# Output and late-query products cut into two 64-row halves that share one PSUM bank, with a TensorE drain between the halves

## The chip, the core and the metric

The kernel runs on one core of a Trainium2 chip. The metric is the device time of one execution in microseconds (us), as the median of several runs. Unless marked ns, all times below are us. Engines are named as the profile names them: PE is TensorE's matmul, PEld its weight load, DVE is VectorE, ACT is ScalarE, POOL is GpSimd, SP is SyncE, which issues most of the DMAs.

## The reference, cut to what matters

Two attention blocks over 2048 tokens of width 512, with 32 heads of 16 dimensions each, are mixed by a gate. Block A is full softmax attention. Block B is causal softmax attention inside four segments of 512 tokens, with a compressive memory of the earlier segments.

```python
x = A_x                                          # [1, 2048, 512]
g = sigmoid((x * gate_w).sum(-1, keepdims=True))
# A: q, k, v = split(x @ A_wqkv) into 32 heads of 16
a = merge(softmax(q @ k.T * 16**-0.5) @ v) @ A_wo
# B: the same inside each segment s of 512 tokens, causal, and a memory of earlier segments
p = softmax(q_s @ k_s.T * 16**-0.5 + causal)
o_s = sig(beta) * (phi(q_s) @ M) / (phi(q_s) @ z + 1e-6) + (1 - sig(beta)) * (p @ v_s)
M, z = M + phi(k_s).T @ v_s, z + phi(k_s).sum(0)
b = merge(o) @ B_wo
out = g * a + (1 - g) * b
```

## The kernel before

All products that need float32 accuracy are made of two numbers for each operand, a high and a low half (`halved[...]`), and three products: low by high, high by low, high by high.

**A first part** (up to about 280 us) computes q, k and v and the memory of block B. A **main part** follows, which is what the change is about. It walks through a list `slots` of 2368 score tiles: 32 units of block A (8 groups of four heads by 4 query chunks of 512), with 64 slots each, and 32 units of block B with 10 slots each. In a slot `n`:

- `score_part` (line 1030) makes one 128x512 score tile with a matmul over 50 rows (line 1045; two smaller matmuls in some slots of B) into a tile `st`, one of three PSUM banks, and lets ACT take the exponential into a tile `p` (line 1068).
- `max_part` (line 263) makes, 96 slots ahead (`LEAD`), a score tile of 48 rows (line 242) into `sm`, one of four PSUM banks, from which DVE takes row maxima (line 275; line 290 for the masked tiles of B). The bank is the one that was read longest ago.

Scores and maxima use 50 and 48 of 64 rows of the TensorE array. Two heads lie in rows 0 to 63 and two in rows 64 to 127 (`rows`, line 199), and the order of slots is such that a score in one half stands beside a maximum in the other.

Three slots make a **burst** (`BURST`). At the end of a burst, the loop (line 1328) gives PE further work:

- normally `some_values` (line 1080), the products of `p` and `v`: matmuls of 128 rows by 17 columns, four heads side by side, that accumulate in one bank, `ops`. When a unit is done, `ops` is copied to `oraw` by ACT (line 1106) and stored.
- if the list `shared` has entries, three of them in place of values. An entry is one matmul of 128 rows, 128 columns and 512 elements into the same bank `ops`, through the helper `matmul` at line 153 (its instructions all show as line 155). Twelve of them make one 128x512 tile, which ACT then copies out of the bank: four bursts for each tile.

`shared` is filled inside `some_values` just after a unit of block A is done, behind the copy to `oraw`. In the first 8 units of A it is filled by `later_tile` (line 958: one 128x512 tile of the queries of chunks 2 and 3), and in 22 later units by `output` (line 1241: 128 rows of the final projection, half of its terms at a time, so that `keep` copies a first half to `part` and `leave` copies the second to `res`). The list is emptied before the unit's successor is done, so that a tile's four bursts follow the unit's end directly.

The order of the instructions of an engine is the order in which this code records them.

Of the kernel before, what the change touches and what calls it, by code (L numbers as in the profile page):

```python
# [10 lines left out]
F32 = mybir.dt.float32  # L11
F32R = mybir.dt.float32r
AF = mybir.ActivationFunctionType
ALU = mybir.AluOpType
# [8 lines left out]
CH = 512  # L23
# [11 lines left out]
LEAD = 96  # L35
BURST = 3
# [3 lines left out]
NP = 6  # L40
# [7 lines left out]
def gated_mix(ctx, tc, x, xT, wqkv, a_wo, b_wq, b_wk, b_wv, b_wo, beta, gate_w, out):  # L48
# [104 lines left out]
    def matmul(*args, **kw):  # L153

        behind[0] = nc.tensor.matmul(*args, **kw)  # L155
# [149 lines left out]
    def run_todo(m):  # L305

        for e in [e for e in todo if e[0] <= m]:
            todo.remove(e)
            e[1]()
# [645 lines left out]
    def x_later(c):  # L955
        return xT[:, c * CH:(c + 1) * CH]

    def later_tile(c, o):

        def done():  # L960
            full = fr.tile([128, CH], F32, tag="part", name="full")
            nc.scalar.copy(full, ops)
            t = fr.tile([128, 2, 2, 2, 128], F32R, tag="blk", name="qhalves", bufs=2)
            t = t.rearrange("p a o h t -> p a (o h t)")
            nc.gpsimd.tensor_copy(t[:, 0], full)
            nc.gpsimd.tensor_sub(t[:, 1], full, t[:, 0].bitcast(F32))
            for i in range(2):
                at(n + 12, lambda i=i: nc.sync.dma_start(
                    qd["A", o, c][16 * i:16 * i + 16].rearrange("d h t -> (d h) t"), raw(t[:, i])))


            if o == NO - 1 and c == LATER[0]:
                for i in range(2):
                    load_halves(("x", LATER[1]), "B", x_later(LATER[1]), (2 * i, 2 * i + 1), n + 2 + 18 * i,
                                [n + 24 + 29 * i, n + 28 + 29 * i])
            elif o == NO - 1:
                for i, (side, w) in enumerate((("A", a_wo), ("B", b_wo))):
                    load_halves(side, side, w, (0, 1), n + 2 + 18 * i, [n + 22 + 8 * i, n + 26 + 8 * i])
                    for k in range(2, 4):
                        load_halves(side, side, w, (k,), n + 50 + 22 * i + 3 * (k - 2), [n + 62 + 18 * i + 5 * (k - 2)])  # L980

        def f(i):
            k, (a, b) = i // 3, ((1, 0), (0, 1), (0, 0))[i % 3]
            assert {("q", k), (("x", c), k)} <= ready
            matmul(ops, halved["q"][:, k, a, o * 128:(o + 1) * 128], halved["x", c][:, k, b],
                             start=(i == 0), stop=(i == 11))
            if i == 11:
                done()
        for i in range(12):
            yield lambda i=i: f(i)  # L990

    vt = {}

# [33 lines left out]

    queue = []

    def score_part(n):  # L1030

        u, j = slots[n]
        side, g, c = u
        q = qt[u]

        if j % 4 == 0:
            pt_[u, j // 4] = pp.tile([128, 4, CH], F32, tag="p", name="p")
            order_p[u, j // 4] = len(order_p)
            assert not queue or order_p[queue[0][1], queue[0][2] // 4] > len(order_p) - 1 - NP
        p = pt_[u, j // 4]  # L1040
        h = (0, 2, 1, 3)[j % 4]

        def score(ps, h, b, k, n0, q0):

            nc.tensor.matmul(ps[:, n0:n0 + CH - q0], rows(k[:, :, b * 128:(b + 1) * 128], h, 50),  # L1045
                             rows(q[:, :, q0:], h, 50), start=True, stop=True)

        def diagonal(x):
            nc.gpsimd.affine_select(out=x, in_=x, pattern=[[0, 4], [1, 128]], base=0, channel_multiplier=-1,  # L1049
                                    compare_op=ALU.is_ge, fill=0.0)  # L1050

        ps = banks[1 + n % BURST] if n in wide and n // BURST % 2 else st_ps.tile([128, CH], F32, tag="st", name="st")
        if side == "A":
            score(ps, h, j // 4 % 4, kt_[u, j // 16], 0, 0)
        else:
            k = kt_[u, c]
            if j < 8:
                score(ps, h, j // 4, k, 0, 128 * (j // 4))
                if j >= 4:
                    score(ps, h, 3, k, 384, 384)  # L1060
            else:
                for f in range(2):
                    score(ps, 2 * (j - 8) + f, 2, k, 256 * f, 256)
        if side == "B" and j >= 8:
            nc.scalar.activation(p[:, 2 * (j - 8):2 * (j - 8) + 2, 0:256], ps.rearrange("p (h t) -> p h t", h=2), AF.Exp,
                                 scale=SCALE)
        else:
            nc.scalar.activation(p[:, h], ps, AF.Exp, scale=SCALE)  # L1068
        if j % 4 == 3 or j == SLOTS[side] - 1:
            if side == "B":  # L1070
                diagonal(p[:, :, 0:128])
                if j == 7:
                    diagonal(p[:, :, 384:])
            queue.extend((n + (2 * BURST * (1 + (side == "B")) if n in wide else GAP[side]), u, i) for i in range(j // 4 * 4, j + 1))


    PIECES = ([(0, 128 * i, 128 * i) for i in range(4)] + [(1, 128 * i, 128 + 128 * i) for i in range(3)] + [(3, 384, 384)]
# [137 lines left out]
    def products(ps, t, b, side, o, start, stop):  # L1215

        assert (side, o) in ready
        for i, (x, w) in enumerate(((1, 0), (0, 1), (0, 0))):
            yield lambda i=i, x=x, w=w: matmul(ps, t[:, b, x], halved[side][:, o, w], start=start and i == 0,
                                                         stop=stop and i == 2)  # L1220

    def out_rows(c, b):
        return out[c * CH + b * 128:c * CH + (b + 1) * 128, :]
# [17 lines left out]
    def output(c, b, pairs, then, ps=ops):  # L1241

        ks = [(os, o, i) for os in pairs for o in os for i in range(2)]
        for k in ks:
            def f(n, k=k):
                os, o, i = k
                assert loaded_blocks[c, b, os] > len(blocks) - 2
                t = blocks[loaded_blocks[c, b, os] - 1][:, i, o % 2].unsqueeze(1)
                list(products(ps, t, 0, "AB"[i], o, k == ks[0], k == ks[-1]))[n]()
                if k == ks[-1] and n == 2:  # L1250
                    then(ps, c, b)
            for n in range(3):
                yield lambda n=n, f=f: f(n)

    part = {}

# [67 lines left out]
        return MOST + (left - 4 >= (MOST + 0.5) * runs and (due > 2 * MOST or runs == 1))  # L1324

    filled = [0]
    n = 0
    while n < nS or queue or beside or filled[0] < len(fill):
        for f in beside.pop(n, []):
            f()  # L1330
        if n < nS:
            score_part(n)
        m = n + LEAD
        if m < nS:
            loads(m + PRE)

            b = oldest()
            max_part(m, lambda: banks[b], b)
        run_todo(m)
        if n >= nS or n % (2 * BURST if n in wide else BURST) == (2 * BURST if n in wide else BURST) - 1:  # L1340
            taken = 0
            if shared:
                for _ in range(3):
                    shared.pop(0)()
            else:
                taken = some_values(n, 8 if n >= nS or n in wide else most(n))
            if n < 5:


# [59 lines left out]
```

## Time and profile before

| | us |
|---|---|
| median of 3 runs | 1745.3 (1744.92 to 1745.94) |
| span of the profiled execution | 1744.5 |
| PE busy | 1738.4 |
| PEld busy | 885.8 |
| DVE busy | 1597.1 |
| ACT busy | 1436.5 |
| POOL busy | 736.5 |

The span reaches from the first to the last instruction of one profiled execution. PE's busy time is no measure of its use, since the ends of matmuls are modelled and matmuls overlap. What a stretch costs is read from the starts of successive matmuls. Rows of the timeline give a start in us from the span's beginning, a duration in us, the engine, the line, the operation, what it writes and reads (with shapes, partitions x elements), how many instructions are merged in the row, and in brackets for how long the engine was idle before and what ended that.

### The profile page before, as it was taken

How to read it: one execution, taken by the hardware profiler on the slowest of the kernel's cores; microseconds unless marked ns; L12 is line 12 of the kernel's file. 1: busy time of each engine (PE TensorE's matmuls, PEld its weight loads, DVE VectorE, ACT ScalarE, POOL GpSimd, SP SyncE). 2: the span in 40 equal slices, each digit the busy share in tenths (PEclk: the TensorE clock that was granted, in tenths of full speed). 3: DMA queues.
4: the chain of work that ended last, by engine and by line, in shares of the span. 5: the costliest groups of instructions: out<-in, count | busy, mean ns of one | idle time of the engine just before them, and what ended most of it. 6: DMA issues, size and time to landing. Idle time of an engine off the chain costs nothing.

```text
span 1744.5 us, 41555 instructions
## 1 busy us (share of the span) xinstructions
PE 1738.4 (100%) x15205; PEld 885.8 (51%) x15205; DVE 1597.1 (92%) x3327; ACT 1436.5 (82%) x2763; POOL 736.5 (42%) x992
## 2 busy tenths in 40 slices
PE   9999999999999999999999999999999999999999
PEld 7887775444444444444444444444444444444445
DVE  7757788999999999999999999999999999999931
ACT  6545557888888898888888888888888888888884
POOL 3543233234352427352534353535344353535443
PEclk9999999999999999999999999999999999999999
DMA  6787567335453446454545454444445444545542
GB/s 209 251 291 227 194 226 215 110 102 145 127 153 105 138 119 183 131 137 136 143 122 157 122 143 130 134 145 122 149 130 148 130 127 124 148 115 147 149 154 63
DMA packets 149387, 261.62 MB, mean 150 GB/s; under 512 B 39064, under 2 KB 61624, under 8 KB 148672
## 3 DMA queue, kind: packets, MB, share of 16 engines
q1 hardware_dynamic: 146640, 254.42, 49.2%
q0 software_dynamic: 2400, 4.29, 0.9%
q8 instruction: 121, 1.98, 0.5%
q14 instruction: 82, 0.67, 0.1%
q10 hardware_dynamic: 144, 0.26, 0.1%
HBM read 174.39 MB, written 83.25 MB: 148 GB/s over the span
## 4 chain that ended last, share of the span: by engine, by line
PE 99%; ACT 0%; DMA 0%; DVE 0%; issue 0%; SPq 0%; ACTq 0%; DVEq 0%
PE ops L155 40%; PE st L1045 28%; PE sm L242 14%; PE pr L366 9%; PE pair L366 4%; PE sm L155 2%; PE mt_ps L232 0%; PE tps L831 0%; PE sm L1045 0%; DMA vs<-wqkv 0%; PE mps L845 0%; PE num L804 0%; PE den L808 0%; ACT p L1068 0%; DVE pm L275 0%
## 5 line engine op out<-in xcount | busy, mean ns | idle before, releaser
L1068 ACT ACTIVATE p<-st 128x512 f32<-128x512 f32 x2261 | 1190.7, 600 | 147.6 <-PE sm L242 98.6
L275 DVE TENSOR_REDUCE pm<-sm 128x1 f32<-128x512 f32 x2048 | 1276.5, 683 | 9.7 <-PE sm L242 8.7
L242 PE MATMUL sm<-kA,qA 48*128 48x512 f32 x2048 | 662.5, 424 | 0.1
L1045 PE MATMUL st<-qA,kA 50*128 50x512 f32 x2014 | 656.2, 432 | 0.0
L155 PE MATMUL ops<-p,vA 128*17 128x256 f32 (+3 forms) x6360 | 553.0, 445 | 0.0
L1045 PEld LDWEIGHTS st<-qA,kA 50*128 50x128 f32 x2014 | 326.8, 185 | 423.4 <-ACT p L1068 378.9
L242 PEld LDWEIGHTS sm<-kA,qA 48*128 48x128 f32 x2048 | 337.8, 185 | 11.3 <-DVE ph L449 3.9
L1169 POOL TENSOR_TENSOR rcp<-rec,minus 128x32 f32<-128x32 f32 x43 | 234.8, 5461 | 78.3 <-DMA rec<-dend 73.5
L290 DVE CUSTOM_DVE_ANT_0 rest<-sm,mask 128x128 f32<-128x128 f32 (+3 forms) x512 | 246.8, 482 | 0.8 <-PE sm L242 0.7
L155 PEld LDWEIGHTS ops<-p,vA 128*17 128x17 f32 x6360 | 129.2, 96 | 216.1 <-issue 185.0
L1049 POOL TENSOR_SCALAR_AFFINE_SELECT p<-p 128x512 f32<-128x512 f32 x128 | 79.4, 637 | 270.4 <-ACT p L1068 265.7
L242 PE MATMUL sm<-kB,qB 48*128 48x128 f32 (+3 forms) x512 | 166.1, 384 | 0.0
L1045 PE MATMUL st<-qB,kB 50*128 50x512 f32 (+1 forms) x495 | 105.4, 330 | 0.3 <-ACT mt L235 0.3
L1045 PEld LDWEIGHTS st<-qB,kB 50*128 50x128 f32 x495 | 68.6, 186 | 62.2 <-ACT p L1068 50.5
L155 PE MATMUL ops<-p,vB 128*17 128x128 f32 (+3 forms) x1504 | 88.3, 350 | 0.0
L242 PEld LDWEIGHTS sm<-kB,qB 48*128 48x128 f32 x512 | 79.9, 184 | 0.0
L214 POOL TENSOR_TENSOR dm<-pm 128x32 f32<-128x32 f32 x32 | 7.9, 247 | 169.9 <-DVE pm L275 169.9
L437 POOL TENSOR_SCALAR mn<-full 128x512 f32<-128x512 f32 x24 | 36.7, 1527 | 75.6 <-ACT full L432 75.6
L223 POOL CAST ms<-pm 128x16 fp32r<-128x16 f32 x32 | 6.3, 196 | 127.5 <-DVE pm L290 127.5
L1185 POOL TENSOR_TENSOR v<-v,inv 128x512 f32<-128x512 f32 x31 | 39.8, 1283 | 28.1 <-DMA inv<-rdA 21.9
L155 PEld LDWEIGHTS ops<-p,vB 128*17 128x17 f32 x1504 | 33.8, 96 | 30.1 <-issue 26.1
L440 DVE TENSOR_TENSOR q<-full,q 128x512 fp32r<-128x512 f32 x40 | 29.2, 731 | 18.6 <-ACT q L433 15.8
(319 smaller groups left out, 1690.9 us busy)
## 6 DMA issues: line engine op xcount, KB each, us to landing
kA<-kdA SPq DMA_DIRECT2D x256, 128.0 KB
vA<-vdA SPq DMA_DIRECT2D x31, 544.0 KB
kA<-kdA SPq DMA_DIRECT2D x256, 64.0 KB
qB<-qdB SPq DMA_DIRECT2D x192, 64.0 KB
kB<-kdB SPq DMA_DIRECT2D x192, 64.0 KB
kdA<-q SPq DMA_DIRECT2D x32, 256.0 KB
qdB<-q SPq DMA_DIRECT2D x32, 256.0 KB
qA<-qdA SPq DMA_DIRECT2D x64, 128.0 KB
```

The costliest lines, as they stand in the source:

```text
L155: behind[0] = nc.tensor.matmul(*args, **kw)
L242: nc.tensor.matmul(ps[:, n0:n0 + n], rows(qt[u][:, :, s * 128:(s + 1) * 128], h, 48), rows(k[:, :, k0:k0 + n], h, 48), start=True, stop=True)
L275: nc.vector.tensor_reduce(pm[:, h, s, kc:kc + 1], ps, axis=AX.X, op=ALU.max, negate=True)
L290: nc.vector.tensor_tensor_reduce(out=tri["rest"][:, 0:w], in0=ps[:, n0:n0 + w], in1=tri["mask"][:, CH - w:], scale=-1.0, scalar=3.0e38, op ...
L366: nc.tensor.matmul(ps, l, r, start=start, stop=stop)
L437: nc.gpsimd.tensor_scalar_min(ph["mn"], full, 0.0)
L440: nc.vector.tensor_sub(q2, full, q1.bitcast(F32))
L1045: nc.tensor.matmul(ps[:, n0:n0 + CH - q0], rows(k[:, :, b * 128:(b + 1) * 128], h, 50), rows(q[:, :, q0:], h, 50), start=True, stop=True)
L1049: nc.gpsimd.affine_select(out=x, in_=x, pattern=[[0, 4], [1, 128]], base=0, channel_multiplier=-1, compare_op=ALU.is_ge, fill=0.0)
L1068: nc.scalar.activation(p[:, h], ps, AF.Exp, scale=SCALE)
L1169: eng.tensor_tensor(r, rec, minus, op=ALU.pow)
L1185: eng.tensor_mul(k["v"], k["v"], k["inv"])
```

## The change

`shared` entries become functions of a row half. Each product of 128 rows is now two matmuls of 64 rows, both into `ops`, so that a tile is 24 matmuls. A burst with `shared` work is recorded by a function of its own, `output_burst`: the three products' halves of one row half, in turn with the scores and maxima that lie in the other row half, and then the three products' other halves, in turn with the remaining scores and maxima. Between the two, where the row half that writes `ops` changes, a `drain` is recorded on TensorE. The next burst starts with the row half that this one ended with. Over the program there are 120 bursts of this kind, 360 matmuls more and 120 drains. `score_part` is cut into three functions (`score_tile`, `score_product`, `score_values`) with the same content. All other bursts stand as before.

```diff
+    def row_halves(l, r, first_, last_, then=None):
+        def half(i):
+            rs = slice(64 * i, 64 * i + 64)
+            halves_done[0] += 1
+            if halves_done[0] > 1 and i != tile_of[0]:
+                nc.tensor.drain()
+            matmul(ops, l[rs], r[rs], start=halves_done[0] == 1, stop=halves_done[0] == 24)
+            tile_of[0] = i
+            if halves_done[0] == 24:
+                halves_done[0] = 0
+                if then:
+                    then()
+        return half
...
     def later_tile(c, o):
...
-            matmul(ops, halved["q"][:, k, a, o * 128:(o + 1) * 128], halved["x", c][:, k, b],
-                             start=(i == 0), stop=(i == 11))
-            if i == 11:
-                done()
+            return row_halves(halved["q"][:, k, a, o * 128:(o + 1) * 128], halved["x", c][:, k, b], i == 0, i == 11, done)
...
+    def score_half(n):
+        u, j = slots[n]
+        return (j - 8) if u[0] == "B" and j >= 8 else j % 2
...
+    def output_burst(n):
+        rows_ = [[], []]
+        for x in range(n, n + BURST):
+            score_tile(x)
+            r = score_half(x)
+            rows_[r].append(lambda x=x: score_product(x))
+            if x + LEAD < nS:
+                rows_[maxs[x + LEAD][1][0]].append(lambda x=x: maximum(x))
+        fs = [shared.pop(0) for _ in range(BURST)]
+        one = turns[0] % 2
+        turns[0] += 1
+        for i, part in ((one, rows_[1 - one]), (1 - one, rows_[one])):
+            for k in range(max(BURST, len(part))):
+                if k < BURST:
+                    fs[k](i)
+                if k < len(part):
+                    part[k]()
+        for x in range(n, n + BURST):
+            score_values(x)
...
+        if shared and n % BURST == 0 and n < nS and n not in wide:
...
+            output_burst(n - BURST + 1)
...
-            taken = 0
-            if shared:
-                for _ in range(3):
-                    shared.pop(0)()
-            else:
-                taken = some_values(n, 8 if n >= nS or n in wide else most(n))
+            taken = some_values(n, 8 if n >= nS or n in wide else most(n))
```

Three places in the order of instructions show what moves. The first is on PE, at the start of the first tile of the final projection. Before, the last values of a unit of A stand first, and the three products of 128 rows stand behind the burst's three scores (`st`) and three maxima (`sm`).

```order
L155 MATMUL ops_3295<-p_9030,vA_8210 17x512 x4
L1045 MATMUL st_9105<-qB01_8072,kB0_200 128x384
L1045 MATMUL st_9105<-qB01_8072,kB0_200 128x128
L242 MATMUL sm2_3293<-kA1_193,qA21_8648 128x512
L1045 MATMUL st_9111<-qB01_8072,kB0_200 128x384
L1045 MATMUL st_9111<-qB01_8072,kB0_200 128x128
L242 MATMUL sm0_3291<-kA1_193,qA21_8648 128x512
L1045 MATMUL st_9117<-qB01_8072,kB0_200 128x384
L1045 MATMUL st_9117<-qB01_8072,kB0_200 128x128
L242 MATMUL sm1_3292<-kA1_193,qA21_8648 128x512
L155 MATMUL ops_3295<-wA_8514,blk_8885 128x512 x3
```

In the change the same place reads as follows, up to the first halves of the burst's products.

```order
L155 MATMUL ops_3295<-p_9158,vA_8322 17x512 x4
L155 MATMUL ops_3295<-wA_8642,blk_9013 128x512
L242 MATMUL sm0_3291<-kA1_193,qA21_8776 128x512
L155 MATMUL ops_3295<-wA_8642,blk_9013 128x512
L1063 MATMUL st_9237<-qB01_8184,kB0_200 128x384
L1063 MATMUL st_9237<-qB01_8184,kB0_200 128x128
L155 MATMUL ops_3295<-wA_8642,blk_9013 128x512
L242 MATMUL sm2_3293<-kA1_193,qA21_8776 128x512
```

The first product into `ops` now stands directly behind the last values, ahead of the burst's scores and maxima. The order does not list the drain, which follows the last row shown.

The second place is on ACT, at the same point. Before, the copy of `ops` to `oraw` is followed by the exponentials of the burst.

```order
L1068 ACTIVATE p_9067<-st_9091 128x512
L1106 COPY oraw_9101<-ops_3295 128x512
L1068 ACTIVATE p_9104<-st_9105 128x512
L1068 ACTIVATE p_9104<-st_9111 128x512
L1068 ACTIVATE p_9104<-st_9117 128x512
```

In the change they stand in the same order.

```order
L1082 ACTIVATE p_9195<-st_9219 128x512
L1136 COPY oraw_9229<-ops_3295 128x512
L1082 ACTIVATE p_9232<-st_9237 128x512
L1082 ACTIVATE p_9232<-st_9246 128x512
L1082 ACTIVATE p_9232<-st_9254 128x512
```

Nothing has moved here: the copy that frees `ops` stands where it stood, while its user on PE has moved ahead.

The third place is on PE at the end of that tile. Before, the tile's last three products are followed by a whole burst of scores and maxima and then by the first values, which write `ops` anew.

```order
L155 MATMUL ops_3295<-wB_8668,blk_8885 128x512 x3
L1045 MATMUL st_9209<-qA11_8007,kA4_196 128x512
L242 MATMUL sm2_3293<-kA2_194,qA21_8648 128x512
L1045 MATMUL st_9214<-qA11_8007,kA4_196 128x512
L242 MATMUL sm3_3294<-kA2_194,qA21_8648 128x512
L1045 MATMUL st_9220<-qA11_8007,kA4_196 128x512
L242 MATMUL sm0_3291<-kA2_194,qA21_8648 128x512
L155 MATMUL ops_3295<-p_9067,vB_8775 17x384 x4
```

In the change the last product half is followed by one more score of its own burst and then by the same burst of scores and maxima.

```order
L155 MATMUL ops_3295<-wB_8796,blk_9013 128x512
L1063 MATMUL st_9350<-qA11_8119,kA4_196 128x512
L1063 MATMUL st_9353<-qA11_8119,kA4_196 128x512
L242 MATMUL sm0_3291<-kA2_194,qA21_8776 128x512
L1063 MATMUL st_9358<-qA11_8119,kA4_196 128x512
L242 MATMUL sm1_3292<-kA2_194,qA21_8776 128x512
L1063 MATMUL st_9364<-qA11_8119,kA4_196 128x512
L242 MATMUL sm2_3293<-kA2_194,qA21_8776 128x512
L155 MATMUL ops_3295<-p_9195,vB_8903 17x384 x4
```

Between the last product and the next values stands one matmul more than before.

68 lines of the change are left out of this document (51 added, 17 removed).

## The prediction

> **What bounds the kernel now.** I read the page first: the busy times, then the chain that ended last.
>
> ```profile
> span 1744.5 us, 41555 instructions
> PE 1738.4 (100%) x15205; PEld 885.8 (51%) x15205; DVE 1597.1 (92%) x3327; ACT 1436.5 (82%) x2763; POOL 736.5 (42%) x992
> PE 99%; ACT 0%; DMA 0%; DVE 0%; issue 0%; SPq 0%; ACTq 0%; DVEq 0%
> ```
>
> PE carries 99% of the chain. That says only that PE never stands still; what it does with the time is read from the starts of matmuls. Next I read the timeline of an ordinary burst, three scores and three maxima with eight matmuls of values behind them.
>
> ```profile
> 700.94 0.50 PE L1045 MATMUL st<-qA,kA 50*128 50x512 f32 x1
> 700.94 0.73 PE L242 MATMUL sm<-kA,qA 48*128 48x512 f32 x2
> 701.28 0.64 PE L1045 MATMUL st<-qA,kA 50*128 50x512 f32 x2
> 701.52 0.40 PE L242 MATMUL sm<-kA,qA 48*128 48x512 f32 x1
> 701.85 1.05 PE L155 MATMUL ops<-p,vA 128*17 128x512 f32 x8
> 702.83 0.50 PE L1045 MATMUL st<-qA,kA 50*128 50x512 f32 x1
> ```
>
> A score and a maximum in opposite row halves start together (both 700.94), so a pair costs one step. The first step of the burst is 0.34 (700.94 to 701.28), the second 0.24 (to 701.52), and the step from the last pair to work of another tile shape is 0.33 (to 701.85). So a change of shape costs about 0.09 when it is made and 0.10 in the step behind it. No row of PE shows a wait for another engine here: PE's own steps set the pace. DVE has little left behind it:
>
> ```profile
> 692.15:737.69 45.54, 45.54 (x394) 19.65 (x390) 45.47 (x97) 40.29 (x79) 17.33 (x26) 1.00 0.47 132
> 728.93 4.28 DVE L275 TENSOR_REDUCE pm<-sm 128x1 f32<-128x512 f32 x7
> ```
>
> In the table of windows DVE (third pair of numbers) is busy for 45.47 of 45.54. Where it has a backlog, seven maxima take 4.28, and with 0.68 for the last that is 0.60 for one step, 1.80 for a burst of three. A burst that PE does much below 1.80 gains only what the four `sm` banks can buffer.
>
> The tiles of `shared` are what the change touches. The groups by form count their matmuls:
>
> ```profile
> L155 PE MATMUL ops<-wB,blk 128*128 128x512 f32 x132 | 42.4, 429 | 0.0
> L155 PE MATMUL ops<-wA,blk 128*128 128x512 f32 x132 | 42.3, 428 | 0.0
> L155 PE MATMUL ops<-wB,wA 128*128 128x512 f32 x96 | 30.8, 429 | 0.0
> ```
>
> That is 360 products, or 30 tiles of 12, or 120 bursts. Three tiles (the first, one of the middle, the last), each from its first burst's start to the start of the next ordinary burst, show that they cost the same:
>
> ```profile
> 321.70:329.06 7.36, 7.36 (x47) 4.75 (x46) 7.36 (x19) 6.54 (x13) 2.49 (x4) 1.00 0.32 92
> 684.45:691.81 7.36, 7.36 (x48) 4.76 (x45) 7.36 (x19) 6.66 (x14) 6.74 (x10) 1.00 0.57 188
> 1632.67:1640.00 7.33, 7.33 (x50) 4.70 (x46) 7.33 (x25) 6.64 (x14) 2.45 (x4) 1.00 0.40 108
> ```
>
> So a tile takes 7.36, a burst 1.84.
>
> **The change, part by part.** I follow the middle tile.
>
> ```profile
> 683.91 0.61 PE L155 MATMUL ops<-p,vA 128*17 128x512 f32 x4
> 684.45 0.44 PE L1045 MATMUL st<-qB,kB 50*128 50x384 f32 x1
> 684.59 0.59 ACT L1106 COPY oraw<-ops 128x512 f32<-128x512 f32 x1
> 685.40 0.96 PE L155 MATMUL ops<-wA,blk 128*128 128x512 f32 x3
> 689.98 0.49 PE L1045 MATMUL st<-qA,kA 50*128 50x512 f32 x1
> 690.31 0.40 PE L242 MATMUL sm<-kA,qA 48*128 48x512 f32 x1
> 690.92 0.96 PE L155 MATMUL ops<-wB,blk 128*128 128x512 f32 x3
> 691.81 0.50 PE L1045 MATMUL st<-qA,kA 50*128 50x512 f32 x1
> 691.97 0.59 ACT L1259 COPY part<-ops 128x512 f32<-128x512 f32 x1
> 692.72 0.52 PE L155 MATMUL ops<-p,vB 128*17 128x384 f32 x4
> ```
>
> *Removed: two changes of shape in each burst.* The three products take 0.89 from their start to the next burst (690.92 to 691.81), in place of three steps of 0.24. The scores and maxima before them take 0.94 (689.98 to 690.92), of which three plain steps, with the masked tiles' extra matmuls, would be 0.76 (0.24 x 3 and 0.04, which is what 1.84 has over the 1.80 of six steps with two changes: 0.34, 0.24, 0.33, 0.34, 0.24, 0.33 less rounding).
>
> *Added: 360 matmuls and their weight loads.* Six product halves stand beside six scores or maxima, in opposite row halves, so a burst is six pairs. A half streams 512 elements like a whole product; I take 0.24 for each pair, the step of the pairs above, and bound it by nothing below that step's rounding; that the halves should not overlap at all is a rival.
>
> *Added: a drain in each burst.* No drain stands inside the main part before. The nearest rows are at the end of the program, where the sequencer reaches a drain early and waits for PE to finish:
>
> ```profile
> L1383 PEldq DRAIN  x2: 13/2145/4277, 1736.3 to 1744.0; - x2
> 1739.73 0.84 PE L155 MATMUL sm<-wA,hl 128*128 128x512 f32 x3
> L1383 PEldq EVENT_SEMAPHORE  x2: 51/51/51, 1743.8 to 1744.4; - x2
> ```
>
> The drain that started at 1736.3 lasted 4.28 and ended at 1740.6, where the last matmul ended too (1739.73 and 0.84: 1740.57). So a drain holds the sequencer until the last matmul is done, which is 0.40 behind that one's start (row 701.52), and some 0.04 more. Then the sequencer has to send on the next weights and matmul, for which I take one of its own steps, 0.05. The step over a drain is then 0.49, and the step behind it 0.34, as behind a change of shape, since no weights can have been loaded ahead. The lower bound is a change of shape, 0.33 (row 701.85), with no extra behind it. For the upper bound I take a full handshake: ACT began to copy 0.68 behind the start of the matmul that it waited for (683.91 to 684.59); a step of 0.70 would be as slow. I take 0.49, which is nearest to the drain's own row.
>
> By the Trainium skill, page "TensorE: Matmul & The Clock Gate", section "Single matmul latency", one matmul of 512 columns alone takes (398 + 512) / 2.4, or 379 ns; the trace gives 0.40 for it, so the page agrees on that part. If the step over a drain were only those 0.38, it would take 13 us off the sum below.
>
> *Sum of the steps of a tile.* First burst: 0.34 + 0.24 + 0.49 + 0.34 + 0.24 + 0.24 = 1.89. The three others start in the same shape, so their first step is 0.24: 1.79 each. Together 7.26, and four times 0.04 for the extra matmuls: 7.42, against 7.36 before. The ordinary burst behind the tile also starts in the same shape and saves 0.10. So the drains eat what the changes of shape gave: -0.04 a tile, 1 us in all.
>
> *Moved: the first product of each tile.* It writes `ops`, and so has to wait for the copy to `oraw`, which reads it. Before, it stood at the end of the burst: the copy was over at 684.59 + 0.59 = 685.18, the product began at 685.40, and the scores and maxima of the burst hid the copy. Now it stands first in the burst, which would start at 684.45. The copy cannot come earlier: it starts 0.07 behind the modelled end of the last values (683.91 + 0.61). So PE stands from 684.45 to 685.18, and 0.07 for the signal (what it took from PE to ACT, though none is shown from ACT to PE): **0.80** in each of 30 tiles. Queued behind the product are the burst's three scores and three maxima, and for these wait ACT and DVE. DVE loses at most the same 0.80, in a round of one tile and its ordinary bursts that grows by as much, so neither falls behind for good, and PE's own 0.80 is the price. It is paid for nothing: the last ordinary burst does not end sooner.
>
> *Moved: the end of the tile.* Before, the copy began at 691.97, 0.09 behind the products' end (690.92 + 0.96), and the values that need the bank began 0.16 behind its end (692.56 to 692.72). Now the copy is over 0.40 + 0.09 + 0.59 = 1.08 behind the last half's start, with the signal 1.15, and the values are due 0.24 x 3 + 0.33 = 1.05 behind it. A wait of 0.10 for each tile.
>
> Moved DMAs: the loads of a burst's three slots are issued with it, up to two slots earlier than before; POOL and SP keep their order, and no wait of PE for a DMA shows in this stretch, so I count nothing.
>
> *Sum.* 0.80 - 0.04 + 0.10 = 0.86 a tile, times 30 is 26 us. On the span of 1744.5 this gives 1770; the runs' median stands 0.8 above the span, so the forecast is **1771**.
>
> **The rivals.**
>
> *A drain as cheap as a change of shape.* For it speaks that a change of shape has to empty the array as well. The step over it is then 0.33 and not 0.49, the one behind it 0.34: 0.64 less a tile, 19 us, which leaves 1752. The Trainium skill, page "TensorEngine Tiling (Array Packing)", section "Key Properties", says that changing the tiling mode drains TensorE, so by that rule an explicit drain would add little to what is removed; the trace agrees with the rule as far as shape changes cost 0.33 and not 0.24.
>
> *Faster than before: the drain also leaves the weights' load hidden.* If the sequencer sends weights on so soon that the step behind a drain is 0.24, another 0.40 a tile go: 0.86 - 0.64 - 0.40 = -0.18, or 5 us less: 1740. It decides for faster once the step over a drain and the one behind it are together below 0.61, against 0.83 in my sum. Against it: behind every change of shape the trace shows 0.34.
>
> *A slow restart.* At 0.70 over the drain, 0.84 more a tile, 25 us: 1796.
>
> *The wait for the copy is hidden anyway.* The time is then the steps alone and the wait at the end: 0.06 a tile, 2 us, 1747. It would need the copy to be over before 684.45, and the values that it reads were not.
>
> *The change doesn't do what it says.* If a product half and its neighbour did not run together, each burst would take six steps of 0.24 more, 1.44, times 120: 173 us, 1944. The pairs of scores and maxima, which lie in the same two row halves and start together, speak against it.
>
> **How the numbers follow.** The forecast gets 0.57, the cheap drain 0.13, the slow restart 0.17, the faster case 0.06, the hidden wait 0.04, no overlap 0.03. A measurement of this kernel tells about 0.2%, or 3.5 us, from no change. Faster holds the faster case, 0.06; the hidden wait and the cheapest edge of the cheap drain (its lower bound comes near 1749) make 0.07 for no change; 0.87 remain for slower. The range runs from 1751, just under the cheap drain, to 1797, the slow restart; outside are the faster case, the hidden wait and no overlap, with the edges of the others.
>
> **What the next profile would show.** Right, if at the first burst of each tile PE idles about 0.8 for `oraw` on ACT, if pairs inside a burst step by 0.24 with a product half and a score starting together, and if one step in each burst is 0.45 to 0.55, with 0.34 behind it. Wrong, if the first product starts without that wait, if the step over the drain is below 0.4 or above 0.65, or if pairs with a product half take more than 0.26 a step.

## The result, and the profile after

| | before | after |
|---|---|---|
| median of 4 runs each | 1745.11 us | 1794.03 us |
| range of the runs | 1744.91 to 1745.94 | 1793.92 to 1794.47 |
| span of the profiled execution | 1744.5 us | 1792.2 us |

The changed kernel is slower: ratio 1.028, 95% interval 1.0265 to 1.0294. The move is 48.9 us. The forecast had the sign, and 1794.0 lies inside its range (1751 to 1797), but it expected a move of 26.

The page of the changed kernel, its first lines and the shares of the chain that ended last:

```profile
span 1792.2 us, 42376 instructions
PE 1742.6 (97%) x15565; PEld 908.0 (51%) x15565; DVE 1611.3 (90%) x3327; ACT 1449.7 (81%) x2763; POOL 737.7 (41%) x992
PE 94%; ACT 4%; issue 1%; DMA 0%; DVE 0%; SPq 0%; ACTq 0%; DVEq 0%
```

PE was busy for 1738.4 us before and is for 1742.6 now, with 360 matmuls more (15205 to 15565): the halves do run beside scores and maxima. But PE no longer carries 99% of the chain, and ACT has 4% of it. The view of waits names what PE waits for (total us, times, longest):

```profile
PE ops L155 <- ACT oraw L1136: 20.9, 30, 0.7
PE st L1063 <- ACT p L1082: 9.6, 20, 0.5
```

Two waits that the kernel before did not have: one in each of the 30 tiles for the copy to `oraw`, which the prediction names, and one in 20 of them for an exponential, which it does not. Their 30.5 us are the stretches in which PE was all idle; a step that is only longer than it should be is not in them.

The timeline of the middle tile (start, duration, engine, line, operation, in brackets the idle time before it and what ended it) shows the first wait:

```profile
695.48 1.05 PE L155 MATMUL ops<-p,vA 128*17 128x512 f32 x8
...
696.60 0.58 ACT L1136 COPY oraw<-ops 128x512 f32<-128x512 f32 x1
...
697.24 0.49 PE L155 MATMUL ops<-wA,blk 64*128 64x512 f32 x1 [0.71 <-ACT oraw L1136]
...
697.24 0.50 PE L242 MATMUL sm<-kA,qA 48*128 48x512 f32 x1
...
697.80 3.98 DVE L275 TENSOR_REDUCE pm<-sm 128x1 f32<-128x512 f32 x6 [0.44 <-PE sm L242]
...
698.08 0.60 ACT L1082 ACTIVATE p<-st 128x512 f32<-128x512 f32 x1 [0.89 <-PE st L1063]
```

The maximum at 697.24 needs no copy; it stands behind the product in the queue, and DVE (idle 0.44) and ACT (idle 0.89) wait for it and for the score.

The timeline of one burst of that tile, around its drain, and the row of the drains (duration min/median/max in ns, on PE's sequencer):

```profile
701.14 0.45 PE L242 MATMUL sm<-kB,qB 48*128 48x128 f32 x2
...
701.49 0.39 PE L155 MATMUL ops<-wA,blk 64*128 64x512 f32 x1
701.66 0.39 PE L242 MATMUL sm<-kA,qA 48*128 48x512 f32 x1
702.16 0.49 PE L155 MATMUL ops<-wA,blk 64*128 64x512 f32 x1
702.16 0.50 PE L1063 MATMUL st<-qA,kA 50*128 50x512 f32 x1
702.49 0.39 PE L155 MATMUL ops<-wA,blk 64*128 64x512 f32 x1
...
702.72 0.39 PE L155 MATMUL ops<-wA,blk 64*128 64x512 f32 x1
```

```profile
L967 PEldq DRAIN  x120: 958/1150/1608, 322.5 to 1685.3; - x120
```

From the last start ahead of the drain to the next start are 0.50 (701.66 to 702.16), then 0.33, then 0.23. The product stream itself stands longer, 701.49 to 702.16, or 0.67: its neighbour, delayed by a masked tile's second matmul (the row of 701.14), ran 0.17 behind it, and the drain waits for both.

The end of the same tile, where the change costs what the prediction did not see:

```profile
704.00 0.49 PE L1063 MATMUL st<-qA,kA 50*128 50x512 f32 x1
...
704.56 0.60 ACT L1082 ACTIVATE p<-st 128x512 f32<-128x512 f32 x1 [0.27 <-PE st L1063]
704.56 0.39 PE L155 MATMUL ops<-wB,blk 64*128 64x512 f32 x1
704.57 0.61 PE L1063 MATMUL st<-qA,kA 50*128 50x512 f32 x2
...
705.05 0.58 ACT L1300 COPY part<-ops 128x512 f32<-128x512 f32 x1
705.20 0.18 PEld L1063 LDWEIGHTS st<-qA,kA 50*128 50x128 f32 x1 [0.44 <-ACT p L1082]
705.21 0.49 PE L1063 MATMUL st<-qA,kA 50*128 50x512 f32 x1
...
705.52 2.08 ACT L1082 ACTIVATE p<-st 128x512 f32<-128x512 f32 x4
706.18 0.50 PE L1063 MATMUL st<-qA,kA 50*128 50x512 f32 x1 [0.48 <-ACT p L1082]
...
706.62 0.84 PE L155 MATMUL ops<-p,vB 128*17 128x384 f32 x8
```

The last product half starts at 704.56, with the tile's last score. The next ordinary burst follows at once and wants three scores in three steps. Its first starts in time (the second matmul of the row 704.57). Its second waits until 705.21, when ACT has read the bank of the score of 704.00 (its weights' load, on PEld, shows the wait), and its third until 706.18: the score of 704.57 is read only behind the copy to `part`. So the values start 2.06 behind the last product half. In the kernel before it took 1.23.

It goes so, within 0.01, in the 20 tiles whose last set of pairs holds two scores. In the ten others the last set holds one score, and the way takes 1.70 to 1.74. One of them:

```profile
797.93 0.39 PE L155 MATMUL ops<-wB,blk 64*128 64x512 f32 x1
...
798.86 0.18 PEld L1063 LDWEIGHTS st<-qA,kA 50*128 50x128 f32 x1 [0.28 <-ACT p L1082]
...
799.21 0.18 PEld L242 LDWEIGHTS sm<-kA,qA 48*128 48x128 f32 x1 [0.17 <-DVE pm L275]
...
799.64 0.52 PE L155 MATMUL ops<-p,vB 128*17 128x384 f32 x4
```

Here one score waits for ACT, and the wait that ends last, just ahead of the values, is that of a maximum for a bank that DVE still reads.

Means over the 30 tiles, worked out from the starts in the traces (us), part the tile at its products:

| | last values to first product | first to last product | last product to next values | sum |
|---|---|---|---|---|
| before | 1.46 | 6.10 | 1.23 | 8.79 |
| after, by the prediction | 1.34 | 7.18 | 1.15 | 9.67 |
| after | 1.29 | 7.28 | 1.94 | 10.52 |

The prediction's row is its own terms: 0.54 to the burst's start and 0.80 of wait; 7.42 less the last step of 0.24; 0.24 x 3 + 0.33 + 0.10. Measured, a tile is 1.72 longer, times 30 is 51.7 us, of which the two ordinary bursts behind it win back 0.09 a tile (1.81 and 1.68 before, 1.67 and 1.72 after), or 2.7 us: 49.0, against the 48.9 of the runs.

### The profile page after: what moved, and what is told of

It reads as the page before. It is cut to its first block, busy times and chain, and to the rows that moved or that the text cites. A ratio compares the mean times of both kernels' runs of the same rounds, so it can differ in the third digit from the quotient of the medians.

```text
span 1792.2 us, 42376 instructions
## 1 busy us (share of the span) xinstructions
PE 1742.6 (97%) x15565; PEld 908.0 (51%) x15565; DVE 1611.3 (90%) x3327; ACT 1449.7 (81%) x2763; POOL 737.7 (41%) x992
## 3 DMA queue, kind: packets, MB, share of 16 engines
q8 instruction: 124, 2.03, 0.5%
## 4 chain that ended last, share of the span: by engine, by line
PE 94%; ACT 4%; issue 1%; DMA 0%; DVE 0%; SPq 0%; ACTq 0%; DVEq 0%
PE ops L155 40%; PE st L1063 24%; PE sm L242 13%; PE pr L366 9%; PE pair L366 4%; ACT p L1082 3%; PE sm L155 2%; ACT oraw L1136 1%; PE mt_ps L232 0%; PE tps L831 0%; PE sm L1063 0%; DMA vs<-wqkv 0%; PE mps L845 0%; ACT part L1300 0%; ACT res L1304 0%
## 5 line engine op out<-in xcount | busy, mean ns | idle before, releaser
L242 PE MATMUL sm<-kA,qA 48*128 48x512 f32 x2048 | 693.9, 424 | 0.1
L1063 PE MATMUL st<-qA,kA 50*128 50x512 f32 x2014 | 673.1, 431 | 9.9 <-ACT p L1082 9.6
L1063 PE MATMUL st<-qB,kB 50*128 50x512 f32 (+1 forms) x495 | 121.8, 325 | 0.3 <-ACT mt L235 0.3
L155 PE MATMUL ops<-wA,blk 64*128 64x512 f32 x264 | 81.8, 415 | 20.3 <-ACT oraw L1136 15.3
L1063 PEld LDWEIGHTS st<-qB,kB 50*128 50x128 f32 x495 | 86.3, 186 | 18.2 <-ACT p L1082 15.2
L155 PE MATMUL ops<-wB,blk 64*128 64x512 f32 x264 | 79.8, 408 | 4.7
L155 PEld LDWEIGHTS ops<-wA,blk 64*128 64x128 f32 x264 | 43.7, 184 | 57.7 <-ACT oraw L1136 35.6
L155 PE MATMUL ops<-wB,wA 64*128 64x512 f32 x192 | 54.8, 411 | 9.1 <-ACT oraw L1136 5.6
```

What stands on the lines that cost most here:

```text
L242: nc.tensor.matmul(ps[:, n0:n0 + n], rows(qt[u][:, :, s * 128:(s + 1) * 128], h, 48), rows(k[:, :, k0:k0 + n], h, 48), start=True, stop=True)
```

## The experiments

The theory that I began with: the forecast's terms hold, and the missing 24 us (0.79 x 30) are waits at the end of the tile. The rivals: drains that cost more than their steps show, and, later, the four banks of the maxima. Ratios are to the kernel before in the same group of runs; it took 1745.1, 1745.7, 1745.7 and 1746.4 us in the four groups, so times of different groups are compared to about 1 us.

**The first burst whole.** The first burst of each tile as before, whole products behind its scores and maxima; the other three with halves and drains. A drain also stands where the second burst's first half follows the whole products, so there are still 120.

```diff
+        if not halves_done[0]:
+            for x in range(n, n + BURST):
+                score_tile(x)
+                score_product(x)
+                maximum(x)
+            for _ in range(BURST):
+                shared.pop(0)(None)
...
+            return
```

> The first burst of each tile does its three products whole and behind the scores and maxima, as before the change; the three other bursts keep the halves and their drains. Theory 'ends of the tile' (the change loses at the two ends of a tile, where ops and the score banks are waited for, and the steps inside about cancel): the wait of the first product, some 0.75 us a tile, goes; the step over the drain that now stands at the second burst instead of nothing takes some 0.1 to 0.2 back; the time falls from 1794 to 1774 (1770 to 1779). Rival 'drains' (the 120 drains are the loss, the wait at the start is caught up later, since VectorE is close to its own limit): the number of drains is the same, the time stays above 1788.

Measured: 1773.95 us, ratio 1.0161 (1.0146 to 1.0176). The 30 waits for `oraw` are gone from the view of waits, and 20 us with them. The term of the first wait is shown. The end of the tile stays long (1.89; 15 tiles now end in each of the two ways), and the kernel is still 28 us above the one before.

**The copy behind the exponentials.** The copy out of `ops` is recorded after the last burst's exponentials, not with the last product half.

```diff
-                if then:
-                    then()
+                if then:
+                    copies.append(then)
...
+        while copies:
+            copies.pop(0)()
         for x in range(n, n + BURST):
             score_values(x)
```

> The copy of ops at the end of a tile is recorded behind the last burst's exponentials and not ahead of the last one; nothing else moves. Theory 'ends': in the 20 tiles in which the last score stands last, its bank comes free about 0.45 us sooner and the next burst's third score waits less; the values then wait a little for the copy; 0.4 us a tile are left, 20 tiles: 1786 (1784 to 1788). In the other 10 tiles nothing changes. Rival 'drains': no change, 1793 to 1795.

Measured: 1790.51 us, 1.0256 (1.0241 to 1.0271), 3.5 below the changed kernel. The mean from the last product to the next values falls from 1.94 to 1.71, but the next ordinary burst grows from 1.67 to 1.77: ACT is still behind, so about half of the gain is given back one burst later.

**Two scores first.** The row half with which a tile starts is chosen so that the set of pairs with two scores comes first in each burst, and the last set holds one. All tiles then end as ten of the 30 did.

```diff
-        one = turns[0] % 2
-        turns[0] += 1
+        one = (len([x for x in range(n, n + BURST) if score_half(x)]) < 2) * 1 if not halves_done[0] else tile_of[0]
```

> In each tile the row half is chosen so that the set of a burst that holds two scores comes first, as it happens in 10 of the 30 tiles of the change; copies and drains stay. Theory 'ends': the 20 other tiles get the shorter end of those 10 (last product to next values 1.72 in place of 2.06 us, and 0.1 inside): 0.45 us x 20 = 9 us, 1785 (1783 to 1788). Rival 'drains': no change, 1793 to 1795.

Measured: 1788.29 us, 1.0243 (1.0226 to 1.026). Right in direction, 3 us short of the expectation: a tile falls by 0.29, or 8.6 us, and about a quarter of it is given back in the second burst behind the tile (1.72 to 1.79). The end is now 1.73 in the mean, with the wait for a bank of the maxima last.

**The drain by itself.** The kernel before with a drain ahead of the three whole products of each of the 120 bursts, where a change of shape stands anyway.

```diff
             if shared:
+                nc.tensor.drain()
                 for _ in range(3):
```

> The kernel before the change with one drain ahead of the three products of each of the 120 bursts, where the tile shape changes anyway: the price of a drain by itself. Theory 'ends', by the prediction's sizes: the step to the first product grows from 0.33 to 0.50 us, the step behind it stays 0.34: 0.17 x 120 = 20 us, 1765 (1761 to 1769). Rival 'drains' (a drain costs the whole loss of 49 us, 0.4 us each, beyond the steps): 1790 or more. If the shape change drains the array as fully by itself: 1745 to 1748.

Measured: 1769.05 us, 1.0135 (1.012 to 1.015): 23.4 us for 120 drains, 0.195 each over a change of shape. The timeline shows two bursts' products, 2.02 apart where the kernel before takes 1.84:

```profile
690.82 0.93 PE L155 MATMUL ops<-wA,blk 128*128 128x512 f32 x3 [0.25 <-ACT p L1068]
...
692.84 0.96 PE L155 MATMUL ops<-wB,blk 128*128 128x512 f32 x3
```

The view puts the idle 0.25 down to ACT; without the drain the products into `ops` show no wait. The step over the drain is 0.49 (median), the forecast's figure, where a change of shape between plain pairs and work of another shape steps by 0.33. At these 120 places, where masked tiles make some steps shorter, the mean step grows from 0.25 to 0.46, and the step behind stays at 0.33. The Trainium skill, page "TensorEngine Tiling (Array Packing)", section "Key Properties", says that a change of the tiling mode drains TensorE; the rival made from it, that an explicit drain adds little to such a change, does not hold here: it adds 0.195.

**No drains, and one bank less for the maxima.** Halves can do without drains if each half sums in a bank of its own. The bank comes from the maxima, three in place of four; the first kernel takes only that bank away, the second also sums the lower row halves there, without drains. (That lower sum is left out of its output.)

```diff
-    read_last = dict(zip(range(4), range(4)))
+    read_last = dict(zip(range(3), range(3)))
...
-            if halves_done[0] > 1 and i != tile_of[0]:
-                nc.tensor.drain()
-            matmul(ops, l[rs], r[rs], start=halves_done[0] == 1, stop=halves_done[0] == 24)
+            halves_of[i] += 1
+            matmul((ops, banks[3])[i], l[rs], r[rs], start=halves_of[i] == 1, stop=halves_of[i] == 12)
+            halves_of[i] %= 12
```

Three banks alone:

> The changed kernel with three banks for the maxima in place of four; the fourth stays empty. It is there to be compared with the next run. Both theories: slower than the change by what VectorE's smaller buffer costs, 0 to 40 us: 1794 to 1834.

Three banks, no drains:

> As the run with three maxima banks, but the products of rows 64 to 127 go to the fourth bank, so that the two row halves never write one bank, and no drain is recorded. That second sum is left out of the output. Theory 'ends': each burst's step over the drain and the one behind it (0.50 + 0.33) become two plain steps (0.24 each), 0.35 x 120 = 42 us less than the run with three banks, as long as VectorE keeps up; the waits at the two ends of a tile stay. If VectorE's 1.80 us a burst is the next limit, 10 to 25 us less. Rival 'drains' (the whole loss of the change is the drains): 49 us less or more.

Measured: 1881.91 us (1.0781, 1.0765 to 1.0797) and 1858.5 us (1.0647, 1.0631 to 1.0663). The missing bank alone costs 88 us, and most of it in bursts that have no products: the ordinary bursts behind a tile go in turn from 1.89 and 1.78 to 1.89 and 2.03. The end of the drains brings 23.4 us, little more than half of the 42 expected, and within the 10 to 25 for the case that DVE limits. That it is the same 23.4 as in the run before is chance: there a drain was added to a change of shape, here it gives way to a plain step. The view of waits, of the first and the second of the two:

```profile
PE ops L155 <- ACT oraw L1136: 21.1, 30, 0.7
PE st L1063 <- ACT p L1082: 9.5, 20, 0.5
```

```profile
PE ops L155 <- ACT oraw L1137: 21.1, 30, 0.7
...
PE st L1064 <- ACT p L1083: 0.2, 1, 0.2
```

Without drains the full stops for an exponential go from 9.5 us to 0.2, but the end of the tile is no shorter: 2.19 in the mean against 2.11. In the 20 tiles the third score still starts about 1.63 behind the last product half, in both kernels, when ACT frees its bank; a late maximum only fills the time in which PE stood still. So the pair does not show that the drain has a part in the wait at the end. And since maxima limit both of these kernels, it does not say what a drain is worth with four banks.

**Both ends whole.** If the wait for `oraw` and the wait at the end of the tile were all, a tile with whole products in its first and last burst, and halves (two drains a tile) in the middle two, would be as fast as before. The edit is that of the first experiment for both ends, with the order of the third and without a drain where whole products and halves meet. The copy stands with the tile's last product, and so behind the burst's exponentials, as in the second.

```diff
+        if halves_done[0] in (0, 18):
+            for x in range(n, n + BURST):
+                score_tile(x)
+                score_product(x)
+                maximum(x)
...
+            return
```

> The first and the last burst of a tile as before the change (whole products behind scores and maxima), the two middle bursts with halves; the set with two scores stands first; no drain where whole products and halves meet, so two drains a tile. Theory 'ends': no wait for ops at either end, the middle bursts cancel, and the last burst saves the 0.10 of its first step, less a wait of up to 0.15 for a score bank: 1745 (1741 to 1750). Rival 'drains': half of the drains are left, so half of the loss: 1770.

Measured: 1771.28 us, 1.0147 (1.013 to 1.0164). The theory missed by 26 us. The rival came near the number, 1770, but the last group of runs speaks against its mechanism. The trace says where: the end of the tile is nearly mended (1.42), but a like loss now stands one burst earlier, between the last half of the third burst and the first whole product of the fourth, 1.67 in the mean, where three steps of 0.24 and one of 0.33, 1.05, would do. In the middle tile:

```profile
694.06 1.89 DVE L275 TENSOR_REDUCE pm<-sm 128x1 f32<-128x512 f32 x3 [0.19 <-PE sm L242]
...
696.36 0.69 DVE L275 TENSOR_REDUCE pm<-sm 128x1 f32<-128x512 f32 x1 [0.17 <-PE sm L242]
696.40 0.40 PE L242 MATMUL sm<-kA,qA 48*128 48x512 f32 x1
696.78 0.18 PEld L1067 LDWEIGHTS st<-qA,kA 50*128 50x128 f32 x1 [0.38 <-ACT p L1086]
696.78 0.50 PE L1067 MATMUL st<-qA,kA 50*128 50x512 f32 x1
...
697.11 0.50 PE L242 MATMUL sm<-kA,qA 48*128 48x512 f32 x1
...
697.54 0.97 PE L155 MATMUL ops<-wB,blk 128*128 128x512 f32 x3
```

DVE idles at 693.87 and 696.19 because the maxima come late; soon after, PE's last maximum of the burst starts only at 697.11, right behind the end of the maximum read at 696.36 (696.36 and 0.69: 697.05). First DVE waits for PE, then PE waits for DVE: the banks of the maxima, which the theory had not counted. The score of 696.78 waits as well, for ACT, so both kinds of bank have a share here; the last group of runs parts them.

**One drain.** As that kernel, with the middle two bursts as one of six products with one drain.

```diff
-            output_burst(n - BURST + 1)
+            width = 2 * BURST if halves_done[0] == 6 else BURST
...
+            output_burst(n - width + 1, width)
```

> As the run with whole products at both ends, but the two middle bursts are recorded as one of six products, all upper or lower halves first, so that a tile has one drain. Theory 'ends': the removed drain is worth 0.35 us a tile, 10 us, if VectorE keeps up: 1735 (1731 to 1743), faster than the kernel before. If VectorE's step of 0.60 us for a maximum limits the tile, no gain over the run with two drains.

Measured: 1773.08 us, 1.0156 (1.0141 to 1.0171): no gain. Its profiled execution has one accident, in the view of waits:

```profile
PE st L1067 <- DMA kB<-kdB: 8.1, 1, 8.1
```

One load comes too late under the new order, in the last of the 30 tiles, and PE stands idle for 8.1 us. That is not all that it costs. In the view of windows (here from 1660 to 1673, just behind the idle time) the number behind the five engines is the granted clock, and it is 0.50:

```profile
1660.00:1673.00 13.00, 13.00 (x65) 7.67 (x67) 8.13 (x23) 7.14 (x13) 8.00 (x5) 0.50 0.09 28
```

The mean granted clock of all four runs is 0.995 to 0.997, where the kernel with two drains has 1.000 in all of its own, so none of them seems free of the accident. From the last values ahead of the tile to the end of the fourth ordinary burst behind it, the tile of the accident takes 28.26, against 16.99 with two drains. In the other 29 tiles that way is 16.84 in the mean, against 17.17: 0.33 a tile, near the 0.35 expected. So taking a drain away, with six products in one run, does pay inside the tile, some 10 us over all tiles, and the accident hides it. A kernel without the accident was not run; an estimate from these numbers is 1761 (1771.28 less 30 times 0.33), still above the kernel before.

**DVE relieved.** To part the two kinds of bank, the unmasked maxima are taken over half the columns, in the kernel before, in the changed one and in the one with whole ends. In a fourth kernel DVE, which then has room, also makes the copies out of `ops` in place of ACT.

```diff
-            nc.vector.tensor_reduce(pm[:, h, s, kc:kc + 1], ps, axis=AX.X, op=ALU.max, negate=True)
+            nc.vector.tensor_reduce(pm[:, h, s, kc:kc + 1], ps[:, :CH // 2], axis=AX.X, op=ALU.max, negate=True)
```

```diff
-            nc.scalar.copy(full, ops)
+            nc.vector.tensor_copy(full, ops)
...
-        return nc.vector.tensor_copy if n > wide.start + 4 else nc.scalar.copy
+        return nc.vector.tensor_copy
...
-        nc.scalar.copy(part[b], ps)
+        nc.vector.tensor_copy(part[b], ps)
```

The kernel before with halved maxima:

> The kernel before, with each unmasked maximum taken over the first 256 of its 512 columns only (the other columns' maxima are left out). DVE's step falls from 0.60 to an estimated 0.35 us, so the four maxima banks come free early. PE carries 99% of the chain before, so both theories expect about 1745 (1740 to 1746). It is the reference for the next three.

The changed kernel with halved maxima:

> The changed kernel with the same halved maxima. Theory 'score banks': the 24 us that my sum lacked at the end of the tiles are waits for the three score banks, which ScalarE empties at its own pace; with DVE relieved nothing changes, 1788 to 1794, 45 to 49 above the halved kernel before. Rival 'maxima banks': DVE, which had 0.04 us to spare in a burst, is what the bunched halves upset; with it relieved only my forecast's 26 us remain: 1765 to 1772.

That, with the copies on DVE:

> As the run before (halved maxima), and the copies out of the output bank (oraw, part, res, full) on DVE, which has room now, in place of ScalarE, so that ScalarE has exponentials only in this stretch. Theory 'score banks': the last score's exponential no longer stands behind a copy of 0.58 us and ScalarE does not fall behind, so about half of the 24 us goes: 1775 to 1783. Rival 'maxima banks': no further change against the run before, within 3 us.

Whole products at both ends, with halved maxima:

> The kernel with whole products in the first and last burst of each tile (1771 us, where 0.62 us a tile are lost between the third burst's last half and the fourth burst's first product) with halved maxima. Theory 'score banks': the loss stays, 1767 to 1771. Rival 'maxima banks': the loss goes, 0.62 + 0.19 us in 30 tiles is 24 us: 1745 to 1750.

| maxima halved in | us | ratio to the kernel before (1746.38) | against the halved kernel before |
|---|---|---|---|
| the kernel before | 1741.99 | 0.9974 (0.9964 to 0.9985) | |
| the changed kernel | 1788.73 | 1.0242 (1.0226 to 1.0257) | +46.7 |
| the same, copies on DVE | 1786.73 | 1.0231 (1.0213 to 1.0248) | +44.7 |
| whole at both ends | 1750.21 | 1.0023 (1.0014 to 1.0032) | +8.2 |

For the changed kernel DVE is not the main cause: relieved, the change still costs 46.7 of its 48.9 us. The 20 longer ends stay at 2.05; the ten shorter ones fall from 1.72 to 1.48. For the kernel with whole ends DVE is most of it: 25.5 us become 8.2. The way from the third burst's last half to the first whole product falls from 1.67 to 1.41; the rest, down to 1.05, stays, and the third score there still waits for ACT. So the theory of the score banks is right for the changed kernel and mostly wrong for the one with whole ends, and the rival the other way round: which banks run out depends on where the halves stand. In the view of waits the changed kernel with halved maxima still has its two waits, 20.9 us for `oraw` in 30 tiles and 9.5 us for an exponential in 20.

With the copies on DVE I expected 1775 to 1783 and got 2 us. The timelines of two tiles' ends show why. First one of the 20 tiles whose last set ends in a score:

```profile
886.34 2.56 ACT L1082 ACTIVATE p<-st 128x512 f32<-128x512 f32 x5 [0.27 <-PE st L1063]
...
886.91 0.68 DVE L1300 COPY part<-ops 128x512 f32<-128x512 f32 x1
886.99 0.49 PE L1063 MATMUL st<-qA,kA 50*128 50x512 f32 x1
...
887.48 0.50 PE L1063 MATMUL st<-qA,kA 50*128 50x512 f32 x1
...
887.91 0.84 PE L155 MATMUL ops<-p,vB 128*17 128x384 f32 x8
```

Five exponentials now run without the copy among them, the third score comes 0.49 behind the second and not 0.97, and the values start 1.57 behind the last product half, 0.48 sooner: so far the theory of the score banks is right. What is left over the forecast's 1.15 is put down to ACT's pace and the 0.27 that it stood idle behind the drain; no run took these away. In the ten other tiles:

```profile
793.58 0.69 DVE L1300 COPY part<-ops 128x512 f32<-128x512 f32 x1 [0.17 <-PE sm L242]
...
794.19 0.41 DVE L275 TENSOR_REDUCE pm<-sm 128x1 f32<-128x256 f32 x1
...
794.66 0.49 PE L242 MATMUL sm<-kA,qA 48*128 48x512 f32 x1 [0.16 <-DVE pm L275]
```

There the copy stands ahead of DVE's maxima, PE waits for a bank of the maxima, and the end grows from 1.48 to about 2.0. And since the copy takes DVE 0.68, not ACT's 0.58, the first product starts 0.11 later in all 30 tiles. On either engine the copy stands ahead of what frees a bank.

## Why the forecast had the sign and half of the size

*First product: right.* Forecast 0.80 of wait in each tile; the mean from the last values to the first product is 1.29 against 1.34, so 0.75. Undoing it brought 20 us.

*The steps: right.* A pair steps by 0.23 (forecast 0.24), the step behind a drain by 0.33 (0.34), and the step over it by 0.495 (median of 120; 0.49): the drain's row ends 0.436 behind the last start, and the next matmul starts 0.06 behind that. What the working did not have is that a drain waits for the slower of two streams: from product to product the four drains of a tile take 0.54, 0.62, 0.64 and 0.57, mean 0.59, where 0.49 and 0.04 for the extra matmuls were counted. With plain steps a little shorter that leaves 0.10 a tile, 3 us. By the Trainium skill, page "TensorE: Matmul & The Clock Gate", section "Single matmul latency", one bf16 matmul of 512 columns alone takes 379 ns. The measured step over a drain, 0.495, is longer by 0.12, so by that figure it is not the matmul's latency alone.

*The drain rivals: wrong.* A drain costs 0.195 more than a change of shape. The cheap drain and the faster case fall by that, and the slow restart (0.70) by the step of 0.495. 1794 is near the slow restart's 1796, but by another mechanism; since that rival set the upper end of the range, it is luck that 1794 lies inside. That halves run beside their neighbours is shown by the pairs' starts, so the no-overlap rival falls too.

*Moved, the end of the tile: mis-sized.* This is the step that failed. It priced the wait for the `ops` bank alone, 0.10; measured, the way from the last product to the next values is 1.94 where the forecast had 1.15, 0.79 a tile or 24 us, and that is the whole gap between 26 and 49 but for the 3 us of the drains, less what is won back. What stood in its place: scores that used to come three at the head of a burst, 0.9 us ahead of its end, now come spread over it, the last with the last pair. The burst behind them wants all three score banks at once. ACT, which needs some 0.48 from one score to the next, stood idle for 0.27 over the drain, and has the copy out of `ops` ahead of the last score. The forecast asked of each moved matmul what it waits for, but not when the bank that it fills comes free for the next burst. That the copy's place has a share is shown by the copy moved behind the exponentials and by the copies on DVE (0.48 in 20 tiles). The halved maxima show that DVE has little part: 0.08 of the 0.79 in the mean, all of it in the ten shorter ends. That the rest is ACT's pace over three banks is read from the waits in the trace; no kernel with a fourth score bank was run. The drain's own share of the 0.79 was not separated with four banks for the maxima.

*Open.* With whole products at both ends some 17 us hang on DVE and its banks. Whether the drains' gaps or the changed order of the maxima starve DVE there was not tried apart. None of the versions of the change was faster than the kernel before.

## What to carry to other kernels

When matmuls are moved inside a loop that runs at PE's pace, price two things for each: what it waits for, and when the engine that reads its result will free the bank for the next round. In this kernel an even spread over a burst was worse than a bunch at its head, because the next burst wanted all banks at once. A copy that was hidden behind other work cost 0.75 us in each tile, more than its own 0.58, once the matmul that needs its bank stood at the head of PE's queue, and what stood behind that matmul stopped with it.

## What the runs showed of the hardware that was not expected

- A drain on TensorE costs 0.195 us over a change of tile shape at the same place (120 drains: 23.4 us in the kernel before). In place of a plain step it costs more: one drain less in a tile, together with six products in one run, was worth 0.33 in the kernel with whole ends.
- Behind 8.1 us in which PE stood idle, the granted clock was 0.50 from 1660 to 1673 (the kernel with one drain).
- Of four banks for the maxima, one less costs 88 us in 1794. DVE is 90% busy in the changed kernel with four banks, and 87% with three.
- The maximum over 256 columns in place of 512 takes DVE 418 ns in place of 683, not half:

```profile
L275 DVE TENSOR_REDUCE pm<-sm 128x1 f32<-128x512 f32 x2048 | 1276.5, 683 | 9.7 <-PE sm L242 8.7
```

```profile
L275 DVE TENSOR_REDUCE pm<-sm 128x1 f32<-128x256 f32 x2048 | 767.0, 418 | 286.2 <-PE sm L242 263.1 <-PE st L1045 23.0
```

These are the groups of the kernel before without and with halved maxima. DVE's idle time there goes from 10 us to 286, and the kernel gains 4.4 us of 1746: here 276 us more of idle time on DVE are worth next to nothing, while in the kernel with whole ends the same relief brings 21.1 us (1771.28 to 1750.21).
